# Attention and feed-forward on one core: masks copied on chip, casts on three engines, and a new order of loads and work

## The chip, the cores and the metric

The kernel runs on one core of a Trainium2 chip. A core has a matrix engine (TensorE, PE in the profile), three engines for elementwise work (VectorE or DVE, ScalarE or ACT, GpSimd or POOL) and a queue engine (SyncE, SP) that issues most of the DMAs. Each engine takes its own instructions in the order in which they are recorded, and semaphores hold an instruction back until its inputs are there. The metric is device time in microseconds (us) from start to end of one execution.

## The reference

Eight batches of eight heads with 576 positions of 64 columns go through attention with a mask, and the joined heads (4608 rows of 512) go through two matrix products with a leaky ReLU between them:

```python
rel = pos[:, None] - pos[None, :]
mask_plain = (rel >= 0) & (rel < 32)
mask_dil = (rel >= 0) & (rel < 128) & (rel % 4 == 0)      # heads 4 to 7
scores = where(mask, q @ k.T / 8, -1e9)
attn = softmax(scores);  x = (attn @ v) as [4608, 512]
h = x @ w_in            # 512 x 2048
out = max(0.01 * h, h) @ w_out   # 2048 x 512
```

Inputs and output are float32 in HBM. The kernel computes in float16 with float32 accumulation.

## The kernel before

**Planner.** The Python code first makes a list of tasks: each has one or several engines with a duration that the author wrote down, its dependencies, and a priority. `_Plan.run` (lines 112 to 175) puts them in an order engine by engine, `_Plan.latest` (177 to 208) gives new priorities from the end backwards, and both are repeated (`ROUNDS`, lines 1550 to 1553). The instructions are then recorded in that order. So a number in the list, such as a duration, changes no instruction by itself, but may change the order of every engine. Numbers at the top (`WHEN`, `RANKS`, `FIRST`, lines 17 to 29) are first priorities and the order of the first loads.

**Order of loads.** All loads and stores go through SP's queue in list order, but for two loads of constants on ACT's queue. `FIRST` names the first 26: `b` and `v` are q/k and v of batch 0, first of the dilated heads, then of the plain ones; `i` is a block of 128 rows by 1024 columns of `w_in` (512 KB; four make the left half, four the right half); `0` is the last 64 positions of batch 0; `c` and `y` are q/k and v of batch 1; `o` is a block of `w_out`; `1` is batch 1's last positions. Loads land in float32 staging tiles (`stg` for q and k, `vst` for v, `wst`, and parts of `gt` and `xt` for weights) and are cast to float16 by `cast` (line 336).

**Attention.** Batches 0 and 1 (`EARLY`) transpose q and k on PE (line 719), copy them from PSUM into `slots` (`move`, line 634) and work in units of 384 columns: scores (862 to 881) into `sps` or `hps`, Exp on ACT (887), the mask either as a bias added on PE before (862) or as a product on DVE after (901), values and sums on PE (913 to 945), reciprocal of the sums as Ln and Exp on ACT (957, 959), and the norm on DVE (963) into `xt`. Batches 2 to 7 transpose on DVE in 32 by 32 blocks (678, 693, 712); for the dilated heads POOL copies from `turned` into `slots` (699, 706). Their 48 units (`late_unit`, line 970 on) are scores (1006), Exp (1019), mask from `late_m` (DVE, 1022), sums and values on PE (1012), Ln and Exp (1030, 1033) and norm (1041). `sides` and the halves of `v_all` that are set to one (`clear_ones`) give the sums.

**Feed-forward.** The 4608 rows go in 12 chunks of 384. For chunks 0 to 7, `up` (line 1069) makes 16 products of 4 matmuls each into `hps` (the first ones into other banks too), and ACT applies the leaky ReLU into `gt` (1080). Chunks 8 to 11 use seven products in place of eight (`up_seven`, 1153). The first four tiles of 128 rows of the second product are plain (`down`, 1240); the other 32 go in eight groups of four, again with seven products in place of eight (`group`, 1331). Results are stored from `osb` and `vst`.

**Filler.** Eight matmuls on a cleared tile `warm` (1450) run at the start, and more are put where the list has gaps before `WARM` = 62 us (1557).

**Masks.** `con` holds the identity, a bias of 480 columns (0 or -60000) and the same 480 columns as 0 and 1 (lines 32 to 51, 360 to 364). The masks of the late units are 1248 columns (lines 54 to 64), loaded into `late_m` ahead of batch 2 (1479 to 1480), though they repeat one pattern of 96 columns and one of 64.

Of the kernel before, what the change touches and what calls it, by code (L numbers as in the profile page):

```python
# [19 lines left out]
WHEN = (17.6, 17.88, 41.53, 55.81, 77.72, 119.79, 137.62, 145.28)  # L20
WARM = 62.0
ROUNDS = 8
PORT = 0.29
C_PORT = 0.27
M_PORT = 0.08
CON = -1484.5
AFTER = -1495.0
FIRST = "bvbviiii0iiiicoocoyoooooy1"
RANKS = ((20.73, 2.5), (-7.56, -3.11), (15.59, 12.18), (-7.15, -2.09))


def _constants():
# [11 lines left out]
    c1 = np.arange(48)[None, :]  # L44
    rel1 = 96 + c1 - (16 + p)
    d1 = (rel1 >= 0) & (rel1 < WIN)
    rel2 = 96 + c1 - np.where((p < 64) & (p % 4 == 0), 128 + p // 4, p)
    d2 = (rel2 >= 0) & (rel2 < WIN)
    masks = np.concatenate([first, band, band, d0, d1, d2], axis=1)
    parts = [ident, np.where(masks, 0.0, -60000.0), masks]  # L50
# [3 lines left out]
def _slot_masks():  # L54

    key = np.arange(128)[:, None] % 64
    rel = np.arange(96)[None, :] - key
    near = (rel >= 0) & (rel < WIN)
    c = np.arange(64)[None, :]
    last = (c // 16 == key % 4) & (c % 16 >= key // 4)  # L60
    parts = [near] * 5
    for u in range(2):
        parts += [near, near[:, 0:80], near, near[:, 0:80], last[:, 32 * u:32 * u + 32]]
    return np.concatenate(parts, axis=1).astype(np.float16)
# [19 lines left out]
class _Plan:  # L84
# [27 lines left out]
    def run(self):  # L112
        for t in self.tasks:
            t.users, t.ready = [], 0.0
        free, waiting = {}, {}
        server = 0.0
        reads = {t for t in self.tasks if t.port and t.choices[0][0] == "POOL" and len(t.choices) == 1}
# [13 lines left out]
        while len(order) < len(self.tasks):  # L131
# [20 lines left out]
            reads.discard(t)  # L152
            if t.port and eng == "DVE" and reads:
                t.dur += C_PORT if t.kind == "cast" else M_PORT if t.kind == "mask" else PORT
# [22 lines left out]
    def latest(self):  # L177
# [10 lines left out]
        while len(rank) < len(self.tasks):  # L188
# [11 lines left out]
            for d in t.deps:  # L200
# [3 lines left out]
                if d.left == 0:  # L204
                    waiting[d.eng].append(d)
        for t, x in rank.items():
            if t.choices[0][0] != "SP" and not t.service:
                t.prio = x
# [3 lines left out]
def kernel(  # L212
# [51 lines left out]
    NMASK = 288 + 96 + 48 + 48  # L264
    NCON = 128 + 2 * NMASK
    NLATE = 480 + 2 * 384
    M_PL, M_D0, M_D1, M_D2 = 128, 128 + 288, 128 + 288 + 96, 128 + 288 + 96 + 48
# [62 lines left out]
    def load(queue, dst, src, n, size, deps, prio, slow=1.0):  # L330
        eng = ENG[queue]
        return plan.dma(queue, {1152 * 128: 0.66, 1152 * 256: 0.95}.get(n * size, 0.45), took(n, size) * slow, deps,
# [31 lines left out]
    t_bias = load("ACT", con[:, 128:128 + NMASK], const_d[:, 128:128 + NMASK], 128, 2 * NMASK, [],  # L364
                  -1498.5)
# [11 lines left out]
    clear_slots(range(4), -2000, [])  # L377
    t_one = clear("POOL", ones, 0.1, 1.0, -1995)
# [3 lines left out]
    def clear_ones(slots, deps, prio=-700):  # L382
        for i in slots:
# [7 lines left out]
    clear_ones(range(2), [], -1980)  # L391
    t_side = [clear("POOL", sides.bitcast(FP32), 0.1, 0.0, -690)]
    t_side += [add("POOL", 0.1, 0.2, t_side[:1],
                   lambda e, h=h: ENG[e].memset(sides[64 * h:64 * h + 64, 64 * h:64 * h + 64], 1.0),
                   -690, 0.0, "set") for h in range(2)]
    late_mask = []
    t_vr = clear("POOL", vst[0][0:64, 1024:2048], 1.0, 0.0, -1970)
    t_vz = clear("POOL", vst[1][0:PAD, 0:D], 0.1, 0.0, -1990)
# [17 lines left out]
    def load_group(b, g, prio, prio_v):  # L416
# [68 lines left out]
        for j in range(2):  # L485
            nn, n_old = ring("NAT", NNAT, n_users := [])
            na, c_qk = nat[nn], []
            for o in range(2):
# [5 lines left out]
                else:  # L494
# [3 lines left out]
                                 CENG if early else ("POOL", "ACT") if b < 4 else ("POOL",)))  # L498
                s_users.append(c_qk[-1])
            if not early:  # L500
# [10 lines left out]
                        (lv if dil else lv[0] + lv[1]) + d_old, prio_v)]  # L511
# [7 lines left out]
    def load_rest(b, prio):  # L519
# [5 lines left out]
        for o, src in ((0, q), (1, k)):  # L525
# [4 lines left out]
                 at(st, 0, 128, 0, [D, 8], [0, 2], [1, D]), 1024, lo + r_old, prio)  # L530
# [7 lines left out]
        for vi in (2, 3, 0, 1):  # L538
            vt, d_users = kept[b, vi]
            c_v = []  # L540
            if vi >= 2:
                c_v = [cast(at(vt, 0, 64, 0, [1024, 2], [128, 4], [1, D]),
                            at(vs, 0, 64, 1024 + (vi - 2) * 256, [512, 2], [D, 4], [1, D]), 512,
                            [lv] + d_users, prio + 30)]
# [5 lines left out]
    def load_w(n, prio):  # L550
# [6 lines left out]
        if n < 8:  # L557
            x = n // 4 * 1024
            src = dram(moe_w_in, n % 4 * 128 * DFF + x, [DFF, 128], [1, 1024])
        else:  # L560
            x = 1024 * (n - 8)
            src = dram(moe_w_out, 128 * x, [2 * DM, 128], [1, 1024])
        t = load("SP", st, src, 128, 4096, old, prio, 1.3 if n < 4 else 1.0)
        for i in range(2):
            if n >= 8:
# [4 lines left out]
                continue  # L570
            g, h = n % 4 // 2, n % 2
# [17 lines left out]
    MOE = 19.71  # L589
# [44 lines left out]
    def move(dst, src, n, deps, prio, eng=("DVE",)):  # L634
# [19 lines left out]
    def turn(b, hp, part, prio):  # L654
# [11 lines left out]
        if b >= EARLY:  # L666
# [7 lines left out]
            for h in range(2):  # L674
                p0 = 64 * h

                def spread(e, c, n, dims, p0=p0):
                    nc.vector.transpose(at(qb, p0, p0 + 64, p0 + c, *dims),  # L678
                                        na[p0:p0 + 64, S + c // 2:S + c // 2 + n])
                if dil:  # L680
                    ev.append(add("DVE", 0.23, 0.2, [c_qk[1]] + old + s_clear[tn],
                                  lambda e, spread=spread: spread(e, 1024, 64, [[1, 64]]), prio))
                else:
                    ev.append(add("DVE", 0.75, 0.2, [c_qk[1]] + old + s_clear[tn],
                                  lambda e, spread=spread: spread(e, 0, S, [[128, 9], [1, 64]]), prio))
            n_users += ev
            if dil:
                for o in (1, 0):
                    xn, x_old = ring("X", 3, x_users := [])
                    xb = turned[xn]  # L690
# [764 lines left out]
    def tick():  # L1455
        clock[0] += 1
        return clock[0]
# [162 lines left out]
```

## Time and profile before

| | before |
|---|---|
| median of three runs | 304.82 us (303.56 to 305.99) |
| profiled execution | 304.83 us |
| its span | 303.0 us |
| granted clock of TensorE | 1.0 |
| PE, DVE, ACT, POOL busy | 96%, 81%, 71%, 43% |
| HBM read, written | 37.68 MB, 9.44 MB |
| filler matmuls | 8 (3.6 us) and 25 (6.8 us) |

The span is measured from the first to the last instruction of the program; the rest of the execution's time lies around it. PE's busy time counts each matmul from start to modelled end, and ends overlap the next start, so it overstates how much of PE's pace is used; filler counts as busy too. An idle time is put down to the semaphore that ended it. In rows of groups, the first number after the bar is the busy time, then the mean of one, then the idle time before them.

### The profile page before, as it was taken

The numbers are of one execution on the slowest core, as the hardware profiler recorded it, in microseconds if no ns is written. First come the engines' busy times: TensorE is split into PE (matmuls) and PEld (weight loads), VectorE is DVE, ScalarE is ACT, GpSimd is POOL, SyncE is SP. The second block draws the span as 40 slices with busy tenths as digits, with TensorE's granted clock in tenths as the row PEclk, the third lists the DMA queues.
The fourth block names the chain that finished last, engine by engine and source line by source line (L and its number), as shares of the span: only waits on it lengthen the run. The fifth ranks groups of instructions, "written<-read, shape, count | busy, mean of one in ns | idle before, by whom it ended". The sixth has DMA issues, their size and how long they took to land.

```text
span 303.0 us, 8093 instructions
## 1 busy us (share of the span) xinstructions
PE 289.6 (96%) x3033; PEld 229.6 (76%) x3033; DVE 246.4 (81%) x485; ACT 214.2 (71%) x523; POOL 129.2 (43%) x175
## 2 busy tenths in 40 slices
PE   5979989999999999999999999899999999999995
PEld 2535655567997788778777786678999999999984
DVE  5859998775999999998988696989998868577662
ACT  3879873697896876875777777466868877877511
POOL 5369876269639648736824745761000000000000
PEclk9999999999999999999999999999999999999999
DMA  7999997989989789558975988973102210031034
GB/s 246 331 331 405 398 366 172 178 164 203 160 164 214 146 159 213 113 133 145 184 153 138 166 174 167 167 185 100 44 2 75 66 35 2 2 107 35 2 110 132
DMA packets 157302, 47.64 MB, mean 157 GB/s; under 512 B 137296, under 2 KB 154576, under 8 KB 157264
## 3 DMA queue, kind: packets, MB, share of 16 engines
q1 hardware_dynamic: 156688, 46.79, 64.9%
q8 instruction: 23, 0.38, 0.5%
q10 hardware_dynamic: 576, 0.35, 0.5%
q14 instruction: 15, 0.12, 0.1%
HBM read 37.68 MB, written 9.44 MB: 155 GB/s over the span
## 4 chain that ended last, share of the span: by engine, by line
PE 69%; DVE 11%; DMA 6%; ACT 5%; SPq 4%; issue 2%; POOL 1%; ACTq 0%; POOLq 0%; DVEq 0%
PE fps L1331 19%; PE hps L1069 17%; PE hps L1153 7%; PE tp L1331 6%; PE fps L1240 5%; SPq L333 4%; PE ops L1153 3%; DMA wst<-in_moe_w_in_dram 3%; PE ops L1012 3%; ACT gt L1080 2%; DVE ee L1022 2%; PE sps L1153 2%; DVE slots L678 2%; DVE turned L693 1%; DVE xt L1041 1%
## 5 line engine op out<-in xcount | busy, mean ns | idle before, releaser
L1069 PE MATMUL hps<-xt,w_in 128*128 128x384 f16 (+1 forms) x556 | 99.5, 307 | 1.5 <-ACT w_in L342 1.3
L1080 ACT ACTIVATE gt<-hps 128x384 f16<-128x384 f32 (+1 forms) x139 | 63.4, 460 | 26.9 <-PE hps L1069 25.8
L1331 PEld LDWEIGHTS <-gt 128*128 128x128 f16 x768 | 72.9, 98 | 9.6
L1069 PEld LDWEIGHTS <-w_in 128*128 128x128 f16 x576 | 49.1, 98 | 23.7 <-issue 2.1
L344 POOL CAST v_all<-vst 64x1152 f16<-64x1152 f32 (+3 forms) x36 | 39.5, 1107 | 19.1 <-DMA vst<-in_v_dram 17.7
L1331 PE MATMUL fps<-w_out,gt 128*128 128x256 f16 x368 | 47.5, 272 | 0.0
L344 POOL CAST nat<-stg 128x576 f16<-128x576 f32 (+1 forms) x49 | 35.0, 736 | 18.8 <-DMA stg<-in_k_dram 10.4
L1041 DVE TENSOR_TENSOR xt<-ops,rc 128x288 f16<-128x288 f32 x48 | 26.8, 558 | 6.6 <-ACT rc L1033 3.6
L1022 DVE TENSOR_TENSOR ee<-ee,late_m 128x384 f16<-128x384 f16 (+1 forms) x48 | 25.0, 530 | 3.2 <-ACT ee L1019 3.1
L678 DVE STREAM_TRANSPOSE slots<-nat 64x64 f16<-64x64 f16 (+1 forms) x48 | 23.9, 498 | 0.5
L1153 PEld LDWEIGHTS <-w_in 128*128 128x128 f16 x256 | 22.1, 98 | 0.5
L1033 ACT ACTIVATE rc<-rc 128x288 f32<-128x288 f32 x48 | 21.3, 449 | 0.5
L1360 ACT COPY stg<-fps 128x512 f32<-128x512 f32 (+1 forms) x24 | 12.9, 536 | 12.3 <-PE fps L1331 10.9
L699 POOL COPY slots<-turned 64x512 f16<-64x512 f16 x24 | 18.9, 788 | 6.2 <-DMA out_dram<-osb 3.2
L693 DVE STREAM_TRANSPOSE turned<-nat 128x576 f16<-128x576 f16 (+1 forms) x24 | 17.6, 738 | 3.4 <-POOL nat L344 2.5
L706 POOL COPY slots<-turned 128x576 f16<-128x576 f16 x12 | 9.8, 818 | 19.2 <-DVE turned L693 18.9
L1012 PE MATMUL ops<-ee,v_all 128*128 128x96 f16 (+2 forms) x240 | 16.4, 199 | 0.5 <-DVE xt L1041 0.5
L1012 PEld LDWEIGHTS <-v_all 128*128 128x128 f16 x240 | 14.7, 98 | 2.9 <-issue 0.7
L1163 ACT COPY rc<-hps 128x384 f32<-128x384 f32 x24 | 11.5, 480 | 7.4 <-PE hps L1153 5.5
L1153 PEld LDWEIGHTS <-stg 128*128 128x128 f16 x192 | 16.5, 98 | 0.3
L1012 PEld LDWEIGHTS <-sides 128*128 128x128 f16 x240 | 14.0, 97 | 3.6 <-issue 0.8
L1331 PE MATMUL fps<-wst,gt 128*128 128x256 f16 x128 | 16.4, 272 | 0.0
(145 smaller groups left out, 594.8 us busy)
## 6 DMA issues: line engine op xcount, KB each, us to landing
stg<-in_q_dram SPq DMA_DIRECT2D x48, 144.0 KB, 3.5
stg<-in_k_dram SPq DMA_DIRECT2D x48, 144.0 KB, 2.9
vst<-in_v_dram SPq DMA_DIRECT2D x12, 288.0 KB, 3.6
vst<-in_v_dram SPq DMA_DIRECT2D x24, 128.0 KB, 2.8
gt<-in_moe_w_in_dram SPq DMA_DIRECT2D x5, 512.0 KB, 7.8
xt<-in_moe_w_out_dram SPq DMA_DIRECT2D x3, 512.0 KB, 10.1
gt<-in_moe_w_out_dram SPq DMA_DIRECT2D x3, 512.0 KB, 9.6
vst<-in_v_dram SPq DMA_DIRECT2D x3, 384.0 KB, 10.2
```

Of the source, the lines that this page charges most:

```text
L344: ENG[e].tensor_copy(out=dst, in_=src)
L678: nc.vector.transpose(at(qb, p0, p0 + 64, p0 + c, *dims), na[p0:p0 + 64, S + c // 2:S + c // 2 + n])
L693: lambda e, xb=xb, o=o, n=n: nc.vector.transpose(xb[:, 0:n], na[:, o * S:o * S + n]),
L699: lambda e, xb=xb, p0=64 * h: ENG[e].tensor_copy(out=at(qb, p0, p0 + 64, p0, [128, 4], [512, 2], [1, 64]), in_=at(xb, p0, p0 + 64, 0, [1, ...
L1012: nc.tensor.matmul(at(bk, 0, 128, o, *dims), stationary(s), et[:, c:c + n], start=i == 0, stop=i == len(parts) - 1, skip_group_check=True)
L1022: lambda e: nc.vector.tensor_tensor(out=et[:, 0:w], in0=et[:, 0:w], in1=mk, op=ALU.mult), prio + 0.1)
L1033: lambda e: nc.scalar.activation(out=rt[:, 0:NQ], in_=rt[:, 0:NQ], func=AF.Exp, scale=-1.0),
L1041: lambda e: nc.vector.tensor_tensor(out=dst, in0=at(ot, 0, 128, 0, *src), in1=at(rt, 0, 128, 0, *src), op=ALU.mult), prio + 0.2)
L1069: nc.tensor.matmul(ht[:, 0:n], at(w_in, 0, 128, i * DFF + j // 2 * 256 + j % 2, [2, 128]), at(xt[m % 2], 0, 128, i * 1152 + x0 + x, [1, n] ...
L1080: lambda e: nc.scalar.activation(out=gt[c % NG][:, j * n_c + x:j * n_c + x + n], in_=ht[:, 0:n], func=AF.Prelu, alpha=0.01),
L1153: nc.tensor.matmul(bk[:, 192 * jj:192 * jj + 192], w(i, 2 * jp + jj), x(i), start=first and jj == 0 and i == 0, stop=jj == 1 and i == 1, s ...
L1331: nc.tensor.matmul(bk[:, x:x + HN], tl[:, off + j * step:off + j * step + 128], rhs(j), start=first and x == 0 and j == 0, stop=j == HJ - ...
```

## The change

- **Masks.** The constants lose the second copy (0 and 1) and two of the patterns; the bias is 336 columns. The 144 columns that batch 1's plain units and small dilated units multiply by are made on ACT as Exp of the bias. `late_m` gets a load of 160 columns early in SP's queue, and six copies on POOL or ACT spread it to 1248.
- **Casts** of q, k and v of batches 0 and 1, of the rest tile and of v's rest may go to POOL, DVE or ACT; copies from PSUM in `move` may go to DVE or ACT everywhere.
- **Slots.** The three pairs of ones in `v_all` are all set at the start (before: two, the third after batch 0), and `warm` is set first on POOL.
- **List.** Durations are changed (issue of a load by its shape, norms, transposes, setting), DVE's extra time is now a wait for POOL's instruction in place of fixed surcharges, the first tasks keep their places, and two of the repeated orderings add random numbers from a seed.
- **Loads.** `FIRST` moves the first `w_in` block ahead of batch 0's first v, the fifth ahead of batch 0's last positions, puts batch 1's q, k and v between the right half's blocks and the first `w_out` blocks, and leaves six `w_out` blocks for the end.

No matmul other than filler is added or taken away; filler goes from 33 to 39 in the new list.

```diff
-WHEN = (17.6, 17.88, 41.53, 55.81, 77.72, 119.79, 137.62, 145.28)
+WHEN = (-23.78, -49.88, 7.42, 71.86, 83.92, 75.08, 124.0, 139.53)
-FIRST = "bvbviiii0iiiicoocoyoooooy1"
-RANKS = ((20.73, 2.5), (-7.56, -3.11), (15.59, 12.18), (-7.15, -2.09))
+W_SLOW = 1.25
+SEEDS = (0, 0, 0, 0, 0, 0, 0, 0, 0, 710924, 334755)
+FIRST = 'bivbviiii0iciicoyoy1oooooo'
+RANKS = ((-10.57, -18.05), (56.51, -21.65), (-14.55, 53.65), (52.82, 20.26))
...
-            if t.port and eng == "DVE" and reads:
-                t.dur += C_PORT if t.kind == "cast" else M_PORT if t.kind == "mask" else PORT
+            if t.port and eng == "DVE":
+                t.dur += max(0.0, free.get("POOL", 0.0) - at)
...
-            if t.choices[0][0] != "SP" and not t.service:
-                t.prio = x
+            if t.prio > -8999 and t.choices[0][0] != "SP" and not t.service:
+                t.prio = x + moved[t.n]
...
-    t_warm = clear("POOL", warm.bitcast(FP32), 0.25, 0.0, -2000)
+    t_warm = clear("POOL", warm.bitcast(FP32), 0.25, 0.0, -9500)
...
-    t_con = load("SP", con[:, 128 + NMASK:NCON], const_d[:, 128 + NMASK:NCON], 128, 2 * NMASK, [],
-                 CON)
+    t_near = load("SP", late_m[:, NLATE - 160:NLATE], late_d, 128, 320, [], NEAR)
+    t_con = add("ACT", 0.21, 0.22, [t_bias],
+                lambda e: nc.scalar.activation(out=con[:, M_KEEP:NCON], in_=con[:, M_BAND:M_KEEP], func=AF.Exp),
+                -700)
+    late_mask = []
+    for to, n_r, step, width, near in ((0, 5, 96, 96, NLATE - 160), (480, 2, 176, 96, 0), (576, 2, 176, 80, 0),
+                                       (832, 1, 32, 32, NLATE - 64), (864, 2, 176, 96, 0), (960, 2, 176, 80, 0)):
+        late_mask.append(add((("POOL", 0.08 + n_r * width * 0.0012), ("ACT", 0.08 + n_r * width * 0.0009)), None, 0.2,
...
-    clear_ones(range(2), [], -1980)
+    clear_ones(range(3), [], -9300)
...
-                                 CENG if early else ("POOL", "ACT") if b < 4 else ("POOL",)))
+                                 W_ENG if early else ("POOL", "ACT") if b < 4 else ("POOL",)))
...
-                        (lv if dil else lv[0] + lv[1]) + d_old, prio_v)]
+                        (lv if dil else lv[0] + lv[1]) + d_old, prio_v, W_ENG)]
...
-    def move(dst, src, n, deps, prio, eng=("DVE",)):
+    def move(dst, src, n, deps, prio, eng=("DVE", "ACT")):
...
-        t_n = add("DVE", 0.52, 0.2, [t_r, t_v] + x_free.get(m, []),
+        t_n = add("DVE", 0.4 if dil else 0.61, 0.2, [t_r, t_v] + x_free.get(m, []),
...
-        if part is None and not late_mask:
-            late_mask.append(load("SP", late_m, late_d, 128, 2 * NLATE, [], tick()))
...
-                    clear_ones((2,), x_done[0, 0][-1:])
...
-    for _ in range(ROUNDS):
-        plan.latest()
+    for seed in SEEDS:
+        plan.latest(seed)
         order = plan.run()
```

The transposes and copies of batches 2 to 7 are written anew (`turned_by` and `put` in the new code, lines 682 to 711) with the same instructions; the copies into `slots` stand at line 687 in place of 699 and 706.

More of the change, by code (lines that the diff above doesn't have):

```diff
@@ L114, in run @@
             t.users, t.ready = [], 0.0
-        free, waiting = {}, {}
+        free, waiting = {}, {e: [] for e in ("PE", "ACT", "DVE", "POOL", "SP")}
         server = 0.0
-        reads = {t for t in self.tasks if t.port and t.choices[0][0] == "POOL" and len(t.choices) == 1}
         def enter(t):
@@ L569, in load_w @@
                 w_out_t[2 * (n - 8) + i] = [c]
-                continue
-            g, h = n % 4 // 2, n % 2
+            return
+        x = n // 4 * 1024
+        t = load("SP", st, dram(moe_w_in, n % 4 * 128 * DFF + x, [DFF, 128], [1, 1024]), 128, 4096, old, prio,
+                 W_SLOW if n < 4 else 1.0)
+        g, h = n % 4 // 2, n % 2
+        for i in range(2):
             for jj in range(2):
@@ L1088 @@
     SEVEN = (8, 9, 10, 11)
-    W_SUMS = 345.35
+    W_SUMS = 171.56
     u_sums, u_last = {}, {}
```

166 lines of the change are left out of this document (78 added, 88 removed).

## The prediction, on record before the run

> **What bounds it now.** I read the page first, then busy time by stretch, then TensorE's timeline for its gaps, then the engine that ended each gap.
>
> ```profile
> span 303.0 us, 8093 instructions
> ...
> PE 289.6 (96%) x3033; PEld 229.6 (76%) x3033; DVE 246.4 (81%) x485; ACT 214.2 (71%) x523; POOL 129.2 (43%) x175
> ...
> PE   5979989999999999999999999899999999999995
> ...
> DMA  7999997989989789558975988973102210031034
> ...
> PE 69%; DVE 11%; DMA 6%; ACT 5%; SPq 4%; issue 2%; POOL 1%; ACTq 0%; POOLq 0%; DVEq 0%
> ```
>
> PE looks full, but its busy time counts latency that overlaps and filler matmuls. So I counted its own work from start to start: eight 128x256 matmuls of L1331 start every 0.87 us and four 128x384 of L1069 every 0.65, both about 2.4 columns per ns. At that pace the widths of all matmuls that are not filler sum to 268 us, in both kernels alike, since the change adds and removes no product. The other 35 us are what a new order can move: 19.6 lie in the first 60 us (40.4 of work is done there), 12 between 60 and 300 (7.9 of that is some 0.02 per switch between small groups, 4.4 are stalls), 3 at the tail, where the stores are the same.
>
> ```profile
> 10.00:20.00 10.00, 8.94 (x87) 4.78 (x86) 7.53 (x22) 9.18 (x27) 4.76 (x6) 1.00 1.06 316
> 20.00:30.00 10.00, 8.54 (x60) 4.65 (x60) 7.87 (x22) 8.23 (x18) 8.58 (x14) 1.00 1.05 389
> 30.00:40.00 10.00, 9.82 (x96) 6.49 (x94) 9.17 (x22) 8.37 (x20) 8.61 (x15) 1.00 1.05 402
> 40.00:50.00 10.00, 9.05 (x71) 4.52 (x69) 9.38 (x23) 5.53 (x15) 6.06 (x9) 1.00 0.83 251
> ```
>
> The columns are PE, its weight loads, DVE, ACT, POOL, granted clock, DMA share and GB/s. From 10 to 40 the DMA share is above 1: loads set the pace. From 30 to 50 DVE is busy 93%, while ACT falls to 5.53 of 10: b=1's plain v, last in the load order, lands at 47.3, so its attention waits.
>
> ```profile
> 22.62 0.50 PE L1069 MATMUL hps<-xt,w_in 128*128 128x384 f16 x2 [1.26 <-ACT w_in L342]
> ...
> 194.48 0.35 PE L1006 MATMUL sps<-slots 128*128 128x96 f16 x5 [1.18 <-POOL slots L699]
> ```
>
> ```profile
> 188.91 1.14 POOL L344 CAST v_all<-vst 64x1152 f16<-64x1152 f32 x1 [0.43 <-DMA vst<-in_v_dram]
> 190.94 1.27 POOL L344 CAST v_all<-vst 64x1152 f16<-64x1152 f32 x1 [0.89 <-DMA vst<-in_v_dram]
> 192.25 2.17 POOL L699 COPY slots<-turned 64x512 f16<-64x512 f16 x2
> ```
>
> The first two rows are the largest stall of the start and the largest of the rest. The last three explain the second: POOL takes its instructions in order, and the copies that PE needs stood behind a cast whose v landed only at 190.8.
>
> **The change, first 60 us.** I walk through the new list (the order on each engine, without times) by PE's work done, W, beside the time at which the old kernel got there. The clock of loads is the old landings: 512 KB each 1.25 us once DMA is full.
>
> *First up-products (W 6.8 to 8.1).* The first w_in load now stands ahead of v: b=0's v lands 1.25 us later (9.25; plain 14.75 for 13.50). Its plain casts were two in a row on POOL (L344, 1.60 from 13.64 to 15.24); now they go to DVE and ACT side by side (0.7), done by about 15.5: 0.3 lost of the 1.25. Behind them the four plain units took 4.8 from there to the last norm (15.24 to 20.0), with three of ACT's w_in casts (0.62 each) between its Ln and Exp in both lists: 20.3, or 20.9 if a cast waits for its load. The w_in quarter that ended the stall landed at 21.92 (the chain of waits has it from 12.62 for 9.30); with one quarter moved ahead and the rest loads moved behind I put it at 20.4, cast by 21.6. So products start 2 later but run through: W 8.1 at 22.5, before 22.6. Gain 0.
>
> *Second half of w_in (W 14.1).* Its last load now has b=1's first q and k ahead of it (2 x 1.25) and lands at 29.3 for 26.98; cast 0.62, products from 30.1, before 30.0. Gain 0.
>
> *b=1.* q and k land 1.8 us earlier, plain v at 38.6 for 47.3, the w_out blocks later: last at 47.3 for 44.6, first two at 35.7. W 21.4, the first down-product, was reached at 37.9; its w_out allows 36.4. W 26.5 was reached at 45.9; there DVE is next: its list from the last norm (20.6) up to the transposes that go with this point holds 54 instructions, by their rows 22.5 us (casts 0.42 to 0.63, the wide ones more, copies 0.22 to 0.43, norms 0.35, masks 0.41), which ends at 43.1 if DVE never waits and at 45.6 if it is busy 90%. The last w_out, wanted at W 33.7, allows 48.0; the old kernel was there at 53.3. So the gain here lies between 0.3 and 2.8 by DVE, and below nothing if PE has no work while the second half of w_in is late (priced as a rival). I take **-1.5**, the middle: ACT, idle for 8.4 us from 40 to 60, can take copies from DVE (a dozen change to it in the new list), but DVE's 93% doesn't fall by itself. On SP each issue takes 0.33 to 0.62, under the 1.25 of its load, so the queue itself costs nothing, except behind v's 256-byte rows, where it stood for 2.95 at 6.41 and 4.32 at 37.04; in the new list most of w_out comes behind the second of these places.
>
> *Edits with no price of their own.* The warm-up's memset goes first on POOL (0.19, it ended PE's first wait at 3.77): eight fillers start near 1 us, but the first transpose waits for q's cast at 4.4 anyway; 0 to -0.3, 0 taken. The third pair of ones (two pairs took 1.70 in L348's row) joins POOL's start, which was done at 4.0 and idle until 5.80: hidden; without cover 0.9. The kept mask is an Exp of 144 columns on ACT before its first cast, idle 2.91 there: hidden. The late masks: a load of 312 KB (4.4 us to landing) becomes 40 KB and six copies, four on POOL (864 columns, by L699's 0.79 for 512 an estimate of 1.3 us) and two on ACT (352 columns, 0.4 by its casts of 512 in 0.62). They stand ahead of or between w_in casts, which DVE and ACT share; taken at 0, 1.3 if they are on the path. The 320 KB less of masks let b=2's loads be issued some 2.5 us earlier, but nothing of b=2 made PE wait.
>
> **The rest.** The 48 late units stand almost where they stood: b=2's 1 to 3 us earlier in W, most others 0.5 to 2.8 later. No instruction changes engine there but a few evictions and one cast. A later place gives the same loads more time, and PE that comes 1.5 us sooner uses that up. In POOL's list of b=7 the second v cast now stands **behind** both copies. So they run from 190.05 (188.91 + 1.14) for 2.17, to 192.2, and PE, which went idle at 193.1, doesn't wait: **-1.3**. The second cast then ends near 193.5; the values that need it were issued at 195.7. The other stalls over 0.3 (81.5: 0.36, 102.1: 0.48, 186.5: 0.68) are DVE's; I leave them, with -1.5 if all go and +2 if the new order makes as many again.
>
> **Sum.** The profiled execution took 304.83 with a span of 303.0; the median of the runs is 304.82, so one serves for both. 304.8 - 1.5 - 1.3 = **302.0**.
>
> [...] The late masks' DVE rows run from 305 to 1308 ns for one shape, median 370. [...]
>
> **Rivals.**
> 1. *Both gains in full.* DVE follows at 43.1 and the four stalls go: -2.8 - 2.9 = 299.1. For: ACT's idle 40 to 60 and the earlier v. Against: DVE was 93% busy even while work was missing.
> 2. *DVE is stretched by POOL.* The new start gives DVE six casts more (two of v's 768 columns, two of 512, two of the rest tile's 1024) beside POOL's. If each w_in and v cast on DVE runs at the 0.63 median of the w_in rows or above, not 0.42, DVE's list is 2 us longer, the start gains nothing, and one more 0.3 stall comes: 304.8 - 1.3 + 0.3 = 303.8. For: 80 to 120, where DVE is busy 96%. Against: ACT takes a dozen of its copies.
> 3. *Slower: the late half of w_in.* Its last two casts stand in POOL's list behind two casts of b=1's q and k, which land at 30.6 and 31.9. So they end near 33.8, and products that were done at 35.4 then start at 34. If q or k land over 1.5 us later than that, PE has little else: 2.3 for the later w_in and 1.3 for POOL's mask copies ahead of its casts, and as PE falls back the 1.3 near 194 goes to another wait: 304.8 + 3.6 = 308.4. It decides once W 18 comes later than 35 (it was reached at 34.6).
> 4. *The list does nothing:* loads decide, and the old stall is only passed on: 304.8; I count it with 2.
>
> **Chances.** Forecast 0.45 (300.7 to 303.2, DVE's bounds), rival 1 0.17, rivals 2 and 4 0.24, rival 3 0.14. A measurement of this kernel can tell about 1% (3 us) from no change. Below 301.8 lie rival 1 and over half of the forecast: faster by over 1% **0.43**; within **0.45**; slower **0.12**. The range leaves out the far half of rival 1 and most of rival 3: **299.4 to 306.4**.
>
> **What would show it.** Right: W 26 near 44 us; ACT over 7 of 10 between 40 and 50; no wait of L1010 on POOL near 190; idle before 60 of 18 us. Wrong: the up-products of j 12 to 15 waiting for a POOL cast near 34 (rival 3); DVE casts above 0.7 on average before 45 (rival 2); a new stall over 1 us after 60.

## The result, and the profile after

| | before | after |
|---|---|---|
| median | 305.48 us (303.56 to 305.99, 6 runs) | 309.55 us (308.75 to 310.25, 6 runs) |
| ratio, with 95% interval | 1 | **1.0143** [1.0112, 1.0174] |
| profiled execution: span | 303.0 us | 307.7 us |
| granted clock of TensorE | 1.000 | 0.994 |

The changed kernel is slower by 1.4%; the forecast was 0.9% faster. Ratios here and below leave out executions that were some 1.5% or more above their kernel's shortest: two of four of x2, one of ten of x11, and a few of the kernel before. The page of the changed kernel, its first lines, busy tenths, and shares of the chain of waits:

```profile
span 307.7 us, 8115 instructions
...
PE 292.6 (95%) x3039; PEld 230.8 (75%) x3039; DVE 249.7 (81%) x476; ACT 223.4 (73%) x541; POOL 123.6 (40%) x173
...
PE   8678789899999999999999999999999999999995
...
PEclk9899999999999999999999999999999999999999
...
PE 81%; DVE 7%; DMA 4%; SPq 4%; ACT 2%; issue 2%; DVEq 0%; ACTq 0%
```

The whole loss stands in the first eight slices of PE's row (60 us), and the clock shows one slice below full. The stretches (columns as in the prediction: PE, its weight loads, DVE, ACT, POOL, clock, DMA share, GB/s):

```profile
10.00:20.00 10.00, 6.63 (x61) 4.31 (x60) 6.67 (x17) 7.05 (x20) 3.27 (x6) 0.83 0.98 262
20.00:30.00 10.00, 8.25 (x67) 4.32 (x66) 5.74 (x17) 8.88 (x23) 5.95 (x11) 1.00 1.03 370
30.00:40.00 10.00, 8.14 (x81) 5.13 (x79) 7.40 (x20) 8.48 (x22) 7.11 (x13) 1.00 1.09 373
40.00:50.00 10.00, 8.88 (x85) 5.25 (x83) 8.45 (x23) 8.72 (x24) 5.82 (x10) 1.00 0.89 311
```

Between 30 and 50 us DVE, which was to be the next limit, is less busy than before (15.85 of 20 us against 18.55), while ACT is busier (17.20 against 13.90): DVE waits. By the prediction's count W (PE's own work done, in us), the two kernels stand like this:

| W | before reached it at | after | after is behind by (before rounding) |
|---|---|---|---|
| 4.05 | 11.97 | 15.16 | 3.2 |
| 8.1 (first up-products done) | 22.6 | 27.5 | 4.9 |
| 18 | 34.6 | 42.2 | 7.6 |
| 37.9 | 57.5 | 65.0 | 7.5 |
| 150 | 175.9 | 182.6 | 6.7 |
| 180 | 208.8 | 213.7 | 4.8 |
| 267 | 298.6 | 303.3 | 4.8 |

So 7.5 us are lost before 60 us and 2.7 come back later. The stall near 194 is one of those that went. The rest of this text is about the first loss. Its two largest places are these, first PE's timeline with the wait ahead of each row in brackets:

```profile
12.18 0.28 PE L929 MATMUL ops<-ee,v_all 128*64 128x96 f16 x4 [2.01 <-DVE v_all L344]
12.29 0.25 PE L917 MATMUL ops<-ee,ones 128*64 128x192 f16 x2
...
12.48 0.37 PE L917 MATMUL ops<-ee,ones 128*64 128x192 f16 x2
...
31.83 0.34 PE L872 MATMUL sps<-slots 128*128 128x96 f16 x4 [0.65 <-DVE slots L648]
...
37.20 0.61 PE L729 MATMUL tp<-con,nat 128*128 128x128 f16 x8 [0.38 <-DVE slots L648]
41.82 0.61 PE L729 MATMUL tp<-con,nat 128*128 128x128 f16 x8 [0.83 <-DVE slots L648]
```

Near 12 us PE waits for the first v, and the matmuls behind the wait run slower (0.37 for a pair that took 0.25). From 31 to 42 us it waits four times for a copy out of PSUM.

### The profile page after: what moved, and what is told of

Read it like the earlier page. It is cut to its first block, busy times and chain, and to the rows that moved or that the text cites. A ratio compares the mean times of both kernels' runs of the same rounds, so it can differ in the third digit from the quotient of the medians.

```text
span 307.7 us, 8115 instructions
## 1 busy us (share of the span) xinstructions
PE 292.6 (95%) x3039; PEld 230.8 (75%) x3039; DVE 249.7 (81%) x476; ACT 223.4 (73%) x541; POOL 123.6 (40%) x173
## 4 chain that ended last, share of the span: by engine, by line
PE 81%; DVE 7%; DMA 4%; SPq 4%; ACT 2%; issue 2%; DVEq 0%; ACTq 0%
PE hps L1073 23%; PE fps L1335 22%; PE tp L1335 8%; PE hps L1157 7%; PE ops L1016 4%; PE fps L1244 4%; SPq L333 4%; PE ops L1157 3%; DMA wst<-in_moe_w_in_dram 3%; PE sps L1157 2%; PE sps L1010 1%; PE sps L1016 1%; PE ops L1010 1%; DMA stg<-in_k_dram 1%; DVE slots L648 1%
## 5 line engine op out<-in xcount | busy, mean ns | idle before, releaser
L1073 PE MATMUL hps<-xt,w_in 128*128 128x384 f16 (+1 forms) x556 | 96.6, 307 | 0.1
L1084 ACT ACTIVATE gt<-hps 128x384 f16<-128x384 f32 (+1 forms) x139 | 62.2, 455 | 20.2 <-PE hps L1073 18.3
L1073 PEld LDWEIGHTS <-w_in 128*128 128x128 f16 x576 | 50.6, 98 | 23.9 <-POOL w_in L344 1.6
L687 POOL COPY slots<-turned 64x512 f16<-64x512 f16 (+1 forms) x36 | 26.2, 728 | 48.4 <-DVE turned L697 31.4
L344 POOL CAST v_all<-vst 64x1152 f16<-64x1152 f32 (+3 forms) x29 | 35.1, 1212 | 5.2 <-PE ops L917 4.1
L1157 PEld LDWEIGHTS <-w_in 128*128 128x128 f16 x256 | 21.9, 98 | 0.3
L717 DVE STREAM_TRANSPOSE slots<-nat 64x576 f16<-64x576 f16 x24 | 18.4, 768 | 0.3
L1244 PE MATMUL fps<-w_out,gt 128*128 128x512 f16 x64 | 16.3, 379 | 1.2 <-DVE w_out L344 1.2
L1321 DVE TENSOR_TENSOR gt<-gt 128x1024 f16<-128x1024 f16 x21 | 17.0, 818 | 0.3 <-PE fps L1335 0.2
```

The costliest lines, as they stand in the source:

```text
L344: ENG[e].tensor_copy(out=dst, in_=src)
L687: lambda e: (nc.scalar.copy if e == "ACT" else nc.gpsimd.tensor_copy)(out=at(to, p0, p1, p0 if to is qb else 0, *dims), in_=at(fr, p0, p1, ...
L717: lambda e, p0=64 * h: nc.vector.transpose(at(qb, p0, p0 + 64, p0, [128, 9], [1, 64]), na[p0:p0 + 64, S:2 * S]), prio))
L1073: nc.tensor.matmul(ht[:, 0:n], at(w_in, 0, 128, i * DFF + j // 2 * 256 + j % 2, [2, 128]), at(xt[m % 2], 0, 128, i * 1152 + x0 + x, [1, n] ...
L1084: lambda e: nc.scalar.activation(out=gt[c % NG][:, j * n_c + x:j * n_c + x + n], in_=ht[:, 0:n], func=AF.Prelu, alpha=0.01),
L1157: nc.tensor.matmul(bk[:, 192 * jj:192 * jj + 192], w(i, 2 * jp + jj), x(i), start=first and jj == 0 and i == 0, stop=jj == 1 and i == 1, s ...
```

## The experiments

Eighteen kernels, each run beside the kernel before. The table has them all; "first v" is when batch 0's dilated v landed, the W columns when that much of PE's work was done (from one profiled execution each; those of x2 and x22 were among their longest, 314.4 and 310.0 us), and the ratio is to the kernel before with its 95% interval. 1% is 3.06 us. Every edit but that of x14 makes the planner write the whole list anew, so two kernels that differ in one line of code differ in the order of much of their work.

| kernel | what it is | ratio | first v | W 8.1 | W 18 | W 37.9 | W 267 |
|---|---|---|---|---|---|---|---|
| before | | 1 | 8.00 | 22.6 | 34.6 | 57.5 | 298.6 |
| after | | 1.0143 [1.0112, 1.0174] | 11.67 | 27.5 | 42.2 | 65.0 | 303.3 |
| x1 | after, first `w_in` behind all of v | 1.0156 [1.0091, 1.0221] | 8.21 | 21.2 | 39.0 | 61.9 | 304.0 |
| x16 | after, first `w_in` two places later | 1.0013 [0.9977, 1.0049] | 9.04 | 24.1 | 38.9 | 60.5 | 300.2 |
| x5 | after, whole load order of before | 1.0066 [1.0042, 1.0090] | 8.71 | 21.5 | 38.1 | 61.3 | 301.0 |
| x3 | after, engines of before | 1.0074 [1.0040, 1.0108] | 11.74 | 26.1 | 39.3 | 62.1 | 301.3 |
| x8 | after, order and engines of before | 1.0026 [1.0001, 1.0050] | 9.97 | 22.5 | 37.9 | 60.6 | 301.1 |
| x9 | as x8, but casts free | 1.0004 [0.9976, 1.0033] | 8.40 | 20.9 | 37.1 | 59.1 | 299.8 |
| x10 | as x8, but PSUM copies free | 1.0073 [1.0037, 1.0109] | 8.15 | 20.9 | 37.2 | 61.4 | 300.6 |
| x17 | after, numbers of before | 1.0139 [1.0089, 1.0190] | 11.50 | 27.7 | 42.3 | 65.2 | 303.7 |
| x18 | after, DVE surcharges of before | 1.0198 [1.0155, 1.0242] | 11.85 | 27.2 | 43.0 | 65.3 | 305.3 |
| x19 | after, priorities of before | 1.0177 [1.0127, 1.0228] | 11.91 | 26.5 | 41.3 | 64.7 | 304.6 |
| x20 | as x16, numbers of before | 1.0172 [1.0130, 1.0214] | 7.94 | 24.7 | 43.5 | 66.9 | 305.0 |
| x2 | before, first `w_in` ahead of v | 1.0161 [1.0073, 1.0248] | 11.77 | 25.8 | 37.9 | 67.5 | 307.2 |
| x4 | before, engines free | 1.0075 [1.0049, 1.0102] | 7.80 | 22.5 | 36.2 | 60.5 | 300.8 |
| x12 | before, changed numbers | 1.0117 [1.0083, 1.0151] | 8.34 | 22.8 | 36.3 | 60.8 | 302.9 |
| x14 | before, two copies ahead of a cast | 0.9999 [0.9963, 1.0034] | 8.27 | 22.7 | 34.6 | 57.6 | 297.9 |
| x11 | before, new masks and slots | 0.9970 [0.9932, 1.0008] | 7.97 | 21.6 | 35.5 | 58.4 | 297.7 |
| x22 | x11, first `w_in` ahead of v | 1.0082 [1.0045, 1.0120] | 12.63 | 27.9 | 39.3 | 61.3 | 303.4 |
| x23 | x11, casts free | **0.9959** [0.9931, 0.9987] | 7.98 | 20.8 | 34.4 | 57.2 | 296.5 |

Theory A was that the first `w_in` load ahead of v is what costs; theory B, that casts and copies out of PSUM, spread over engines, queue behind other work and wait for each other. C, D, E and F are told where they come up.

### The load order and the engines, each put back or done alone

x1, x2 and x5 change one line, x1 and x5 of the changed kernel, x2 of the kernel before:

```diff
-FIRST = 'bivbviiii0iciicoyoy1oooooo'
+FIRST = 'bvbviiiii0iciicoyoy1oooooo'     # x1
+FIRST = "bvbviiii0iiiicoocoyoooooy1"     # x5: as before
...
-FIRST = "bvbviiii0iiiicoocoyoooooy1"
+FIRST = "bivbviii0iiiicoocoyoooooy1"     # x2
```

x3 takes the freedom of engines away; x4 gives the same freedom to the kernel before:

```diff
-    def move(dst, src, n, deps, prio, eng=("DVE", "ACT")):
+    def move(dst, src, n, deps, prio, eng=("DVE",)):
...
-                                 W_ENG if early else ("POOL", "ACT") if b < 4 else ("POOL",)))
+                                 CENG if early else ("POOL", "ACT") if b < 4 else ("POOL",)))
...
-                        (lv if dil else lv[0] + lv[1]) + d_old, prio_v, W_ENG)]
+                        (lv if dil else lv[0] + lv[1]) + d_old, prio_v)]
```

> The changed kernel, with one step of the load order undone: the first w_in block is no longer ahead of batch 0's first v; the rest of the new order stays. Theory A (loads): that block delays v by 3.7 us (11.67 for 8.00) and the plain v by as much, and nearly all of the 6.3 us that the first up-products lost comes from it: the last norm of batch 0 ends near 23 instead of 26.3, the time falls by about 3.5, to 306. Theory B (engines): the casts and PSUM copies that now go to DVE and ACT stand behind other work and wait for each other, and the load only filled time that was lost anyway: the last norm near 25.5, the time 308.5 to 309.5.

> The kernel before, with the same one step done alone: the first w_in block goes ahead of batch 0's first v, all else as before. Theory A: the first v lands 3 to 4 us later, the last norm of batch 0 ends near 23.5 instead of 20.0, the time rises by about 3.5 to 309. Theory B: 1.25 us of landing, of which most is hidden: 305 to 306.5.

> The changed kernel, with the free choice of engines undone: casts of batches 0 and 1 go to POOL or DVE, v and the rest tile to POOL, PSUM copies to DVE but for the few that had ACT before. The load order and the rest stay new. Theory A: the late v stays, so the time stays within 1 of 309.5. Theory B: v is cast on POOL as it lands and no copy waits for another engine's copy: the last norm near 23, the time near 306.5.

> The changed kernel with the whole load order of the kernel before; engines, masks, slots and list stay new. Theory A: the start is back (last norm near 20.5) and what the later part won, 2.7 us from W 38 on, stays: 302.5 to 304. Theory B: the start stays 2 to 3 us late: 306 to 307.5.

Neither theory held alone: x1 (310.3 us) and x5 (308.0) came out above both ranges that were named for them, and x3 (308.0) between its two. Order and engines put back singly each gave back half of the loss (x5: 0.8%, x3: 0.7%). x1 won 6.3 us at W 8.1 and lost all of them again: 3.1 by W 18, in waits for PSUM copies, for ACT and one for `w_in`, and 3.8 more between 60 us and the end, in many small waits that I can't put down to one cause. x2 is slower than before by 1.6%. Its four executions took 308.9 to 314.4 us, and the shortest is what theory A had (309). In the one profiled, the longest, there is a second loss, which was not expected; its DVE and POOL timelines:

```profile
38.55 6.26 DVE L901 TENSOR_TENSOR ee<-ee,con 128x384 f16<-128x384 f16 x1 [1.15 <-ACT ee L887]
```

```profile
37.87 1.16 POOL L344 CAST w_out<-wst 128x512 f16<-128x512 f32 x2
...
41.76 1.17 POOL L344 CAST v_all<-vst 128x512 f16<-128x512 f32 x2
42.88 1.72 POOL L344 CAST w_out<-gt 128x512 f16<-128x512 f32 x3
```

A mask product of 0.36 us took 6.26, until 0.2 us behind the end of a row of twelve casts that POOL had ready one behind the other (three of its five groups are shown), and PE stood for 5.0 us behind it; the granted clock of this execution was 0.989, and a pair of 128x192 matmuls at 47.79 took 0.52, where x11's pairs of that shape took 0.33. At W 267 this execution is behind by 8.6 us; without the wait it would be 3.6, near the 3.2 that it was behind at W 8.1. Whether the 308.9 us execution had the long mask too is not known, since it has no profile.

### Both put back, and the engines split into casts and copies

x8 is x3 with the load order of before; x9 frees the casts in it again (the lines with `W_ENG` above), x10 the copies out of PSUM (the line of `move`). Theory C: two causes that add; theory D: any new list loses 2 to 4 us somewhere.

> The changed kernel with the load order of before and with the engines of before for casts and PSUM copies; masks, slot clearing, list costs and list ranks stay changed. Undone singly, each gave only 1.5 us back, the order by 6 us at the first up-products and the engines between 14 and 18 us of PE work. Theory C, two causes that add, each with a loss of its own: 18 us of PE work done at 34 to 36 us (before 34.58, after 42.16), 37.9 at 57 to 59, and the rest as in the changed kernel, so 301.5 to 304 us in all. Theory D, any new list loses 2 to 4 us somewhere and the two undone parts are not the cause: 305.5 to 309 us, with the loss behind 38 us of PE work.

> The changed kernel with the load order of before and PSUM copies back on DVE; the casts may still go to any of three engines. If the freed copies out of PSUM are what loses between 14 and 18 us of PE work: 302 to 304 us, as with both back. If it is the freed casts: 306.5 to 308.5 us, and 18 us of PE work at 37 to 38 us.

> The changed kernel with the load order of before and the casts back on their two engines; the PSUM copies may still go to ACT. If the freed copies out of PSUM are what loses: 306.5 to 308.5 us and 18 us of PE work at 37 to 38 us. If it is the freed casts: 302 to 304 us.

> The kernel before with nothing changed but the engines that casts and PSUM copies may go to. Theory C: slower than before by 1 to 3 us, 306.5 to 308.5, and 18 us of PE work done at 36 to 38 us (before 34.58). Theory D, or a freedom that harms only beside the new load order: 304 to 306 us.

With both back 1.2% of 1.4% is gone; singly they gave 0.8% and 0.7%, so within the intervals they add. But x8's 306.4 us lie in theory D's range and not in C's, and it reached W 18 at 37.9, not at 34 to 36, so something else slows the start (with the old numbers, x11 below, it is 35.5). x9, at 305.4, fell between its two ranges. Of the engines it is the **copies out of PSUM** that cost: freed, they make x9 into x5 (0.6%, the intervals don't meet) and x8 into x10 (0.5%, the intervals overlap a little). On the kernel before, with nothing else changed, casts and copies freed together cost 0.75% (x4). Freed casts cost nothing in either pair. The copies' trace from 10 to 50 us, before, after, and in x9 (groups that read the bank `tp`, then what its users waited for):

```profile
L640 DVE COPY slots<-tp x32: 167/356/692, 11.5 to 45.2; 64x128 f16<-64x128 f16 x8, 64x384 f16<-64x384 f16 x4, 64x512 f16<-64x512 f16 x4, 128x512 f16<-128x512 f16 x4
...
  DVE slots L640: 0.5, 2
```

```profile
L648 DVE COPY slots<-tp x22: 167/355/674, 15.4 to 48.0; 64x128 f16<-64x128 f16 x5, 64x512 f16<-64x512 f16 x4, 64x32 f16<-64x32 f16 x4, 64x480 f16<-64x480 f16 x3
L646 ACT COPY slots<-tp x10: 208/474/586, 15.8 to 47.2; 64x128 f16<-64x128 f16 x3, 128x512 f16<-128x512 f16 x3, 64x384 f16<-64x384 f16 x2, 64x64 f16<-64x64 f16 x1
...
  DVE slots L648: 3.7, 6
  ACT slots L646: 3.5, 6
  PE tp L729: 1.6, 3
```

```profile
L648 DVE COPY slots<-tp x32: 167/350/692, 11.7 to 45.9; 64x128 f16<-64x128 f16 x8, 64x384 f16<-64x384 f16 x4, 64x512 f16<-64x512 f16 x4, 128x512 f16<-128x512 f16 x4
...
  PE tp L729: 0.7, 1
```

On one engine the 32 copies follow each other. On two, twelve of the 32 wait until the other engine's copy from `tp` has ended: 7.2 us of idle time on DVE and ACT, and 1.6 on PE. The common target `slots` alone does not order them: in the changed kernel none of the 22 copies from `tp` on DVE overlaps one of the ten on ACT, while a copy from `tp` and one from `fps` overlap (ACT's from `tp` at 16.72 for 0.47 us beside DVE's from `fps` at 16.61 for 0.67), both into `slots`. The planner's list has no such dependency, so in it the copies run side by side. Two rows of DVE's timeline in the changed kernel show how that grows: its copy waits for ACT's, which stood behind an Exp, a Ln and leaky ReLUs, and eight transposes wait for it each time (the rows at 37.20 and 41.82 above).

```profile
36.73 0.42 DVE L648 COPY slots<-tp 64x512 f16<-64x512 f16 x1 [1.07 <-ACT slots L646]
...
40.82 0.86 DVE L648 COPY slots<-tp 64x512 f16<-64x512 f16 x2 [1.07 <-ACT slots L646]
```

### Masks, numbers of the list, one stall, one place in the queue

x11 is x8 with the list's numbers of before, so the kernel before with new masks, slots and ones. (In x11, x17, x20, x22 and x23 a few durations of the list stay new: the issue of a load, transposes and setting; so do the fixed places of the first tasks.) x12 is the kernel before with the numbers alone (the lines of `WHEN`, `RANKS`, `SEEDS`, `W_SLOW`, `MOE`, the norms' durations, and DVE's wait for POOL). x16 is the changed kernel with one letter of `FIRST` moved:

```diff
-FIRST = 'bivbviiii0iciicoyoy1oooooo'
+FIRST = 'bvbiviiii0iciicoyoy1oooooo'     # x16
```

The numbers, as x12 has them on the kernel before (x17 and x11 the other way round; `MOE`, `W_SUMS`, `SUMS` and the norm's duration go with them); x18 puts back only the two lines on DVE, x19 all but these, `W_SLOW` and the norm's duration:

```diff
-WHEN = (17.6, 17.88, 41.53, 55.81, 77.72, 119.79, 137.62, 145.28)
+WHEN = (-23.78, -49.88, 7.42, 71.86, 83.92, 75.08, 124.0, 139.53)
-ROUNDS = 8
+SEEDS = (0, 0, 0, 0, 0, 0, 0, 0, 0, 710924, 334755)
+W_SLOW = 1.25
...
-            if t.port and eng == "DVE" and reads:
-                t.dur += C_PORT if t.kind == "cast" else M_PORT if t.kind == "mask" else PORT
+            if t.port and eng == "DVE":
+                t.dur += max(0.0, free.get("POOL", 0.0) - at)
```

x14 is the kernel before, where after planning batch 7's second v cast gets its place on POOL behind the copies that PE waits for:

```diff
+    pool = [t for t in order if t.eng == "POOL"]
+    for c in late_v[B - 1]:
+        i = n = pool.index(c) + 1
+        while n < len(pool) and pool[n].port and not pool[n].kind:
+            n += 1
+        if n > i:
+            c.start = pool[n - 1].start + 0.001
```

> The kernel before with one instruction moved: in batch 7 POOL takes the second v cast behind the two copies of 64x512 that PE waits for near 194 us. Every other engine keeps its order. If the forecast's second step holds by itself: the stall of 1.34 us at 194.5 goes, nothing late takes its place, and the kernel is 1.3 us faster than before (ratio 0.996). Rival, the stall is only passed on: ratio 0.999 to 1.001, with a new stall of about 1 us between 194 and 215.

> The kernel before with the new masks (Exp on ACT, a load of 160 columns in the first queue, six copies), all slots and ones set at the start, and the rewritten copies of the late batches; the load order, the engines and every number of the list as before. If these edits cost nothing, as the forecast had it: 305 to 306.5 us and 18 us of PE work at 34.6 to 35.5. If the mask load among the first w_in loads, or the mask copies among the casts, cost time: 306.5 to 308 us, and 18 us of PE work past 36.5.

> The kernel before with the changed numbers of the list alone (priorities, durations of norms, DVE's wait for POOL, the two random seeds); load order, engines, masks and slots as before. If the list's numbers carry the gain seen behind 60 us of the changed kernel: 302.5 to 304.5 us. If they were good only for the changed kernel's own start: 305.5 to 308 us, with new stalls in place of the old four.

> The changed kernel with its first w_in load behind batch 0's first v and the second q and k, but still ahead of the plain v. In the changed kernel the dilated v landed at 11.67 us (before 8.00), PE stood still for 2.17 us and the granted clock fell to 0.83 from 10 to 20 us; the plain v landed at 17.10 (before 13.50). If the late dilated v and the clock are the larger part: first up-products at about 23 us (8.1 us of PE work; changed kernel 27.5, before 22.6), clock 1.0, 308 to 308.5 us in all. If the plain v decides: 8.1 us of PE work at 25 to 26.5, and 309 to 310 us.

**x14**, the forecast's second step by itself. POOL's timeline of x14:

```profile
189.32 1.14 POOL L344 CAST v_all<-vst 64x1152 f16<-64x1152 f32 x1 [0.17 <-DMA vst<-in_v_dram]
190.41 2.23 POOL L701 COPY slots<-turned 64x512 f16<-64x512 f16 x2
192.58 1.61 POOL L344 CAST v_all<-vst 64x1152 f16<-64x1152 f32 x1
```

The copies start at 190.41 (the forecast said 190.05) and PE's wait near 194 is gone, but a wait of 0.52 near 187 is 1.02 in this execution; PE is 0.6 us ahead at the end, and in times nothing can be told (0.9999). **x11**: masks and slots cost nothing, as forecast. **x16**: two places in the queue are worth 1.3%, and with them the changed kernel is level with before; its 306.1 us are below both ranges that were named. **x12**: the numbers alone cost 1.2%, of which the forecast knew nothing; its 309.2 us are above both ranges.

### Do the numbers cost in the changed kernel? And do the causes add?

x17 puts the same numbers of the list back in the changed kernel, x18 only DVE's fixed surcharges, x19 only priorities and repeated orderings; x20 is x17 with x16's load order.

> The changed kernel with every number of the list as before (priorities, repeated orderings without seeds, DVE's surcharges, norm durations, the factor of the first w_in loads); load order, engines, masks and slots stay changed. Theory E, the numbers cost here as they did on the kernel before: 305.5 to 307.5 us. Theory F, the numbers suit the new load order and the freed engines, and these two are the loss: 309 to 312 us.

> The changed kernel with one number back: DVE's extra time in the list is again a fixed surcharge of 0.08 to 0.29 us in place of a wait until POOL's instruction ends. If this model is what spoils the list (it holds DVE back by up to a whole POOL cast): 306 to 308 us. If it does not matter: 308.5 to 310.5 us.

> The changed kernel with its first priorities and its repeated orderings back (eight, without seeds) and the modelled wait of DVE for POOL kept. If the priorities spoil the list: 306 to 308 us. If they do not matter: 308.5 to 310.5 us.

> The changed kernel with the first w_in load two places later (as in x16, which took 306.1 us) and every number of the list as before. If the two causes add (3.4 us for the place of the load, about 2 to 3 for the numbers): 302 to 304.5 us, faster than before. If the list only scatters: 305 to 308 us.

They don't: x17 is where the changed kernel was, and with half of the old numbers it is no better (x18 and x19, at 311.8 and 311.1 us, above both of their ranges). Theory E (they cost here too) falls for the changed kernel, though they cost 1.2% on the kernel before and 0.6% between x11 and x8. x20 was to be the fastest and is slow, and a single row of DVE explains it:

```profile
38.17 4.19 DVE L910 TENSOR_TENSOR ee<-ee,con 128x384 f16<-128x384 f16 x1
```

POOL had seven casts ready one behind the other from 37.98 to 42.15. The mask ended 0.2 us behind them, and PE stood for 3.4 us; the granted clock was 0.83 from 40 to 50. So x20 against x17 says nothing on the place of the load: its 3.0 us at W 8.1 were lost here.

### The place of the first w_in load, and the casts, on the fastest version

```diff
-FIRST = "bvbviiii0iiiicoocoyoooooy1"
+FIRST = "bivbviii0iiiicoocoyoooooy1"     # x22, nothing else differs from x11
```

x23 is x11 with the four casts of `load_group` and `load_rest` free to go to POOL, DVE or ACT.

> The version with masks only (x11, 304.3 us), with its first w_in load ahead of batch 0's first v and nothing else changed. If the place of this load is the main cause: dilated v landed at 11.5 to 12 us in place of about 8, plain v at 16.9 to 17.4, 8.1 us of PE work at 25.5 to 27.5 (x11: 21.6), 308 to 310.5 us in all. If it costs only beside the other parts of the change: 305 to 306.5 us.

> The version with masks only (x11, 304.3 us), with the casts free to go to any of three engines; PSUM copies as before. If freed casts gain (on the changed list with the old load order they gave 1.0 us, x9 against x8): 302.5 to 304 us, faster than before. If they queue behind other work as the plain v's did in the changed kernel: 305.5 to 307 us.

One load, moved from behind all of v to ahead of it, costs 1.1% (3.4 us; the intervals don't meet), and its path is in the trace. PE in x22:

```profile
13.42 0.37 PE L936 MATMUL ops<-ee,v_all 128*64 128x96 f16 x4 [3.27 <-POOL v_all L349]
...
14.53 0.61 PE L734 MATMUL tp<-con,nat 128*128 128x128 f16 x4
```

The first v lands 4.7 us later, PE stands for 3.3, the left half's last `w_in` quarter is cast from 25.9 on in place of 21.6, and W 8.1 comes 6.3 later. In this execution 3.4 of that is won back by W 37.9 and 2.8 lost again by W 267, of which one wait for POOL near 176 is 1.1. **x23** is faster than before by 0.4% [0.1%, 0.7%], and so the one version here that beats both: 304.4 us beside 306.0 for the kernel before in the same runs. Its casts were not slower or later than in x11 (W 8.1 at 20.8 against 21.6).

## Why the prediction was wrong, step by step

**First up-products: "Gain 0". This step failed, and most of the loss is here.** Its time for v ("b=0's v lands 1.25 us later (9.25; plain 14.75 for 13.50)") was mis-sized: 3.67 later for the first (11.67) and 3.60 for the plain one (17.10). A block of 512 KB was priced by the pace of a full queue. The packets say what was left out: when the first v landed, 2.04 MB had been moved before and 2.97 after, that is 0.52 of the block and 0.41 of loads issued behind v; and from 5 to 12 us the queue moved less, as the two pages of that stretch show (before, then after); why it did is not shown:

```profile
DMA packets 4213, 2.44 MB, mean 348 GB/s; under 512 B 2397, under 2 KB 4213, under 8 KB 4213
```

```profile
DMA packets 1856, 2.16 MB, mean 309 GB/s; under 512 B 136, under 2 KB 1728, under 8 KB 1856
```

The prediction then priced the plain v alone. The first v it noted with its time and gave no consequence: PE stood for 2.0 us, and the clock fell (0.83 from 10 to 20 us). And the casts, "done by about 15.5", side by side as soon as v landed, were queued behind other work on the two engines that took them, while POOL was idle from 14.46 to 19.13: DVE cast at 18.39, ACT from 19.67 to 20.49.

```profile
18.39 0.54 DVE L344 CAST v_all<-vst 128x768 f16<-128x768 f32 x1
```

```profile
19.67 0.82 ACT L342 CAST v_all<-vst 128x768 f16<-128x768 f32 x1
```

A second landing was mis-sized by more. The last `w_in` quarter of the left half, which the prediction put at 20.4, landed at 25.47 (before: 21.92); from 10 to 20 us the queue moved 262 GB/s, before 316. DVE had its cast ahead of the last norm, whose input ACT had ready at 24.71, and the products waited for that norm:

```profile
25.49 0.42 DVE L344 CAST w_in<-wst 64x512 f16<-64x512 f32 x1 [1.68 <-DMA wst<-in_moe_w_in_dram]
25.95 0.36 DVE L967 TENSOR_TENSOR xt<-ops,rc 128x192 f16<-128x192 f32 x1
```

```profile
26.36 0.65 PE L1073 MATMUL tp<-xt,w_in 128*128 128x384 f16 x3 [1.33 <-DVE xt L967]
```

With the load two places later (x16) v, the plain v and this quarter landed at 9.04, 15.74 and 21.31, and W 8.1 came 3.4 us earlier, so most of the 4.9 goes with the place of the load (on x11 it was 6.3). How it divides between the late v, the clock and the late quarter is not shown: x3, with casts and copies as before, v as late and the clock at 1.00, was 1.4 us better, but there the quarter also landed 2.2 earlier, at 23.28.

**Second half of w_in (W 14.1): "Gain 0".** From W 8.1 to 14.1 it took 8.1 us where the forecast had 7.6. Right but for the late start.

**b=1: "-1.5". Wrong in sign.** From W 14.1 to 26.5 the kernel took 16.3 us, before 15.4 to 15.9 (PE stood from 30.0 to 30.5 at W 14.1): 2.5 were lost by W 18, and some of that came back. Plain v, put at 38.6, landed at 42.61, but no wait of PE over 0.3 us was for it. The forecast took DVE for the limit and let ACT's idle time relieve it. ACT did take copies (it was busy 8.72 of 10 between 40 and 50, as "over 7 of 10" had it), but none of those from the bank `tp` ran beside one on DVE: the dozen copies that it counted as relief are copies that wait for each other, 7.2 us in all between ACT and DVE. By x9 and x5 this is worth 0.6%. Copies of 64 partitions wait for each other here too (ACT's at 31.05 for 0.88 us, DVE's at 31.34 for 0.33). With these waits the second engine added handovers and no pace to the copies from `tp`, and that should have been weighed.

**"The late half of w_in" (rival 3), "308.4": the right side for another reason.** W 18 came at 42.2, past its 35. But between 30 and 42 us no up-product waits over 0.3 us for `w_in`; the waits are those for PSUM copies.

**Order on POOL in batch 7: "-1.3". The stall went, the gain was half.** No wait for POOL near 190 is left in the changed kernel. Alone (x14) the step made 0.6 us in the profile and nothing that the times can tell, since a wait just ahead of it grew.

**Edits at no price.** Masks, slots and ones: right as far as the times can tell (x11). The list's numbers were not among them at all. They move no instruction's duration, and in the changed kernel they cost nothing (x17), but on the kernel before 1.2% (x12). How much of a list's effect is the number and how much the accident of one order stays open: x17 to x20 say that it cannot be read from one change alone.

**The signs that were named.** W 26 was to come near 44 us and came at 51.4; the idle time before 60 us was to be 18 and is 26.9 (33.1 of work is done there); no new stall over 1 us came after 60, the longest wait there is 0.4.

**DVE stretched by POOL (rival 2).** Once in the changed kernel: a cast of `w_out` that takes 0.41 us took 1.66, beside two casts on POOL from 55.49 to 56.66, and PE stood 1.20 us for it.

```profile
55.28 1.66 DVE L344 CAST w_out<-gt 128x512 f16<-128x512 f32 x1
```

```profile
56.99 1.24 PE L1244 MATMUL fps<-w_out,gt 128*128 128x512 f16 x5 [1.20 <-DVE w_out L344]
```

Its other instructions before 60 us were stretched by 0.44 at most, and the early masks took 0.34 to 0.75. The stretch was priced far too low, as x2 and x20 show: not 0.2 us a cast, but once a mask product of 6.26 us and once one of 4.19, for 0.36. (The late masks' rows that the prediction names are of two shapes, 384 and 416 columns, not one.)

**What adds up.** Walking back from the changed kernel: load order 0.8% (x5), then engines 0.4% (x8), then numbers 0.6% (x11), and masks less than nothing. In another order the shares differ: engines first give 0.7% (x3), numbers first nothing (x17). So they are no constants of the parts. What is shown as one edit on otherwise equal code, list planned anew, is the place of the first `w_in` load (x22, and x16 on the changed kernel) and the copies out of PSUM (x9 against x5). Even there the size hangs on the rest of the list: x1 moves the same load still further back and gains nothing.

## What to carry to other kernels

A load moved ahead in a queue that was just filling up cost the one behind it more than its own size over the full pace: the first v came 3.67 us later for a block of 512 KB that was priced at 1.25. Price such a load at the first instruction that PE waits for, the clock included. Before a copy is let go to a second engine, look where it reads: from `tp` two engines only took turns here, and the queue of each became the other's wait (7.2 us). And a long unbroken row of casts on POOL was a risk for the mask products on DVE: beside such rows one took 6.26 us (x2) and one 4.19 (x20) in place of 0.36.

## What the runs showed of the hardware

- **Two mask products on DVE ended only with a row of casts on POOL.** They took 6.26 us (x2) and 4.19 us (x20) in place of 0.36 and ended 0.2 us after POOL's row of casts did, twelve of them in x2 and seven in x20.
- **The clock fell after a stand of 2.0 us.** In the changed kernel matmuls went from 0.25 to 0.37 us a pair within 0.3 us of the end of a stand of 2.01 us, and four transposes took 0.61, in x11 0.39; the granted clock was 0.83 over 10 to 20 us. It was 0.66 over the same stretch in x22, with a stand of 3.27 us, and 0.83 over 40 to 50 us in x20, with one of 3.42. x1, which stood for 1.53 us ahead of 28.54, kept 1.00 in its profiled execution.
